# The channel mix over 12 blocks of 384 tokens instead of 9 of 512

## The chip, the core and the metric

The kernel runs on one core of one Trainium2 chip. The metric is the device time of one execution in microseconds (us); lower is better. The core's engines are named as the profile names them: PE (matrix products; PEld is its loading of weights), DVE (vector engine), ACT (scalar engine), POOL and SP, which issues the DMAs.

## The reference, cut to what matters

There are 8 batches of 576 tokens, 8 heads of 64, so a token has 512 channels. Attention goes through 32 packed rows per head, and its output feeds a channel mix:

```python
def attention(q, k, v, p):                 # 8 batches, 8 heads, 576 tokens, 64 wide
    packed = sm_attn(p, k, v)              # 32 packed rows over 576 tokens
    return sm_attn(q, packed, packed)      # 576 tokens over 32 packed rows

def channel_mix(x, mu_k, mu_r, w_k, w_v, w_r):     # x: 8 x 576 tokens x 512 channels
    x_prev = shifted_by_one_token(x)               # zeros ahead of each batch
    xk = mu_k * x + (1 - mu_k) * x_prev
    xr = mu_r * x + (1 - mu_r) * x_prev
    k = maximum(xk @ w_k, 0)                       # 512 -> 1024
    v = (k * k) @ w_v                              # 1024 -> 512
    return sigmoid(xr @ w_r) * v
```

## The kernel before, in words

**Precision.** Every operand of the mix's three products is kept as two fp32r parts, high and low, and every product is three matmuls: high x high, high x low, low x high. The weights are split once (`convert`, L267 to L299): DVE does the integer steps L287, L289, L291 and the subtraction L297, ACT does L285 and L295. There are 20 such pieces: 4 of w_r, 8 of w_k, 8 of w_v.

**Attention, batch by batch.** `loads` and `transposed` bring k and q (L364 on DVE, or L387 on PE for the first two batches), `front` and `weights_of` make the packed rows (L437, L504, L510, L520, L461, L476), and `back` (L541, L553 to L576, L584) makes the batch's output, which ACT copies to SBUF (L606). Attention's DVE rows are mostly 576 elements wide and do not depend on the block of the mix.

**The mix, block by block.** The 4608 tokens are one row of tokens, cut into NB blocks of TB tokens, across the borders of batches. A block i needs every batch of which it holds a token:

- `mix` makes xr and xk, four chunks of 128 channels each: a product with mu on ACT (L639), a multiply-add on DVE (L643), both in one piece for each batch that the block holds; then `split` makes the two parts, ACT L659 and DVE L661.
- `gates`: for each of NT = TB / 128 tiles of tokens, 4 chunks x 3 matmuls (L717 to L719). The 128 tokens are the weights that PE loads, the 512 output channels stream, so a matmul is 128x512 whatever TB is. ACT makes the sigmoid (L728).
- `keys`: for each of 8 tiles of 128 hidden channels, 4 chunks x 3 matmuls (L678 to L680). Here the 128 hidden channels are the weights and the TB tokens stream, so a matmul is 128 x TB. `squared` follows: ACT relu L689 and square L692, DVE L696 and L698.
- `values`: 8 hidden tiles x NT token tiles x 3 matmuls of 128x512 (L746 to L748); `done` multiplies by the gate on DVE (L757) and writes 128 tokens out.

PE's order for a block is gates, keys, values; the mix of block i + 1 is begun when the keys of block i are done (`channel_mix`, L763 to L771).

**What sets the order.** Nothing is scheduled by the hardware beyond each engine's queue. `Flow` plans the program as it is built: every part (a Python generator) names the engine and an assumed duration for its next instruction (`pe(0.69)` for three matmuls), and the planner records whichever part can start first, with ranks for ties. Each engine then executes its own list strictly in that order and waits where an input is missing. So assumed durations choose an order, and the chip's durations decide the time. Until the last gate tile of block 0 is planned, PE gets filler products (L817) in planned gaps.

**Buffers around the change.** Four buffers `xk`, eight `sq` (for squared keys, xr and staged weights), four `tmp` of 512, four `sig`, and four PSUM banks `m` for the products of the mix.

Of the kernel before, what the change touches and what calls it, by code (L numbers as in the profile page):

```python
# [163 lines left out]
def attn_pack_channel_mix(ctx: ExitStack, tc: tile.TileContext, q, k, v, p, mu_k, mu_r, w_k, w_v, w_r, out):  # L164
    nc = tc.nc
    B, H, S, D = q.shape
    NP = p.shape[2]
    DM, DF = w_k.shape
# [5 lines left out]
    NQ = 4 * P  # L174
    NC = DM // P
    NF = DF // P
    TB = 512
    NB = B * S // TB
    NT = TB // P
    WP = 512  # L180
# [21 lines left out]
    def pe(us, after=None):  # L202
        return "tensor", us, after, None
# [29 lines left out]
    def tile_(shape, dtype, tag, slot, name=None):  # L233
        return sb.tile(shape, dtype, name=name or tag, tag=f"{tag}{slot}")
# [7 lines left out]
        for j in range(2 if tag != "free" else 1):  # L242
            const.tile([P, 1 if "m" == tag[0] or "n" == tag[0] else 2], F32, name=f"{tag}{j}", tag=f"{tag}{j}")
    for tag, n, size in (
        ("xk", NC, 2 * TB), ("sq", NF, 2 * TB), ("tmp", 4, WP), ("sig", 4, DM), ("kq", 4, S), ("a", 2, S),
        ("raw", 3, S), ("a2", 1, S), ("e", 2, S), ("aT", 1, 5 * P), ("vt", 2, NPR * 4 * D),
    ):
        for j in range(n):
            sb.tile([P, size], F32, name=tag, tag=f"{tag}{j}")
# [365 lines left out]
    def pieces(i):  # L615
        t, end = i * TB, (i + 1) * TB
        while t < end:
            b, s = divmod(t, S)
            n = min(S - s, end - t)
            yield b, s, n, t - i * TB  # L620
            t += n
# [3 lines left out]
    def mix(i, j, res, tag):  # L625
# [3 lines left out]
        for c in range(NC):  # L629
# [4 lines left out]
            sx = yield from flow.take(space)  # L634
            x32 = tile_([P, TB], F32, space, sx, "x32")
            ready = flow.t
# [31 lines left out]
    def keys(i):  # L668
        for f in range(NF):
            slot = yield from flow.take("m")  # L670
            ph = ps.tile([P, 512], F32, name="ph", tag=f"m{slot}")[:, :TB]
            fs = slice(f * P, (f + 1) * P)
            for c in range(NC):
                yield from flow.wait(("xk", i, c), ("wk", c, f * P // WP * WP))
                yield pe(0.69)
                flow.now.t -= flow.LAG
                _, xh, xl = xks[i, c]
                nc.tensor.matmul(ph, wk_h[:, c, fs], xh, start=(c == 0), stop=False)  # L678
                nc.tensor.matmul(ph, wk_h[:, c, fs], xl, start=False, stop=False)  # L679
                nc.tensor.matmul(ph, wk_l[:, c, fs], xh, start=False, stop=(c == NC - 1))  # L680
                if f == NF - 1:
                    flow.give("xk", xks.pop((i, c))[0])
            flow.spawn(squared(i, f, slot, ph), 0, flow.t + flow.LAG)

    def squared(i, f, slot, ph):
        sr = yield from flow.take("tmp")
        r = tile_([P, WP], F32, "tmp", sr, "r")[:, :TB]
        yield act(TB)
        nc.scalar.activation(r, ph, AF.Relu)  # L689
        flow.give("m", slot)  # L690
        yield act(TB)
        nc.scalar.activation(r, r, AF.Square)  # L692
        sh = yield from flow.take("sq")
        hl = tile_([P, 2, TB], F32R, "sq", sh)
        yield vec2(TB)
        nc.vector.tensor_copy(hl[:, 0, :], r)  # L696
        yield vec(TB)
        nc.vector.tensor_tensor(hl[:, 1, :], r, hl[:, 0, :].bitcast(F32), op=ALU.subtract)  # L698
        flow.give("tmp", sr)
        sqs[i, f] = sh, hl  # L700
        flow.set(("sq", i, f))
# [61 lines left out]
    def channel_mix():  # L763
        for i in range(NB):
            if i == 0:
                mixes(i)
            yield from gates(i)
            yield from keys(i)
            if i + 1 < NB:
                mixes(i + 1)  # L770
            yield from values(i)  # L771
# [74 lines left out]
```

## Time and profile before

| what | before |
| --- | --- |
| median of 3 runs | 606.17 us (605.31 to 607.71) |
| span of the profiled execution, first to last instruction | 605.1 us |
| median less that span | 1.1 us |
| mean granted PE clock | 0.997 |
| PE busy | 593.7 us (98%) |
| DVE busy | 363.9 us (60%) |
| ACT busy | 331.0 us (55%) |
| matmuls of the mix | 2160, all of them 128x512 |

The profiled execution has no separate time of its own beside its span, so the 1.1 us stands for what lies around it. Times in the trace count from the first instruction. A timeline row gives the start, the length of the merged run, the engine, the line, the operation, output <- inputs, the shape and the count; brackets give idle time before it and what ended that. A matmul's length in such a row is its way through the pipeline: the distance between two starts is what it costs in a stream. A row of stretches gives for each engine its busy time and its number of instructions, then the granted PE clock.

### The profile page before, as it was taken

What the parts mean: (1) busy time and instruction counts of PE and PEld (TensorE: products, weight loads), DVE (VectorE), ACT (ScalarE), POOL (GpSimd) and SP (SyncE); (2) the same over time, 40 slices, a digit from 0 to 9 for tenths busy, and PEclk for the clock granted to TensorE, in tenths of its full rate; (3) what the DMA queues carried; (4) which work ended last, traced back from release to release, by engine and by line L of the source; (5) the groups of instructions that cost most, each with busy time, mean ns of one, the idle gap of its engine ahead of it and who ended that gap; (6) DMA issues with size and microseconds to landing.
All of it is one profiled execution on the core that took longest, in us unless ns stands there. A gap on an engine that the chain in (4) does not pass through costs nothing.

```text
span 605.1 us, 10174 instructions
## 1 busy us (share of the span) xinstructions
PE 593.7 (98%) x3984; PEld 471.1 (78%) x3984; DVE 363.9 (60%) x701; ACT 331.0 (55%) x579; POOL 2.1 (0%) x23
## 2 busy tenths in 40 slices
PE   8899999999999999999999999999999999999997
PEld 7787777777777777777877787778788888888886
DVE  1499999949688479556765577166503822451321
ACT  4478784775774648454845485457534803641420
POOL 0000000000000000000000000000000000000000
PEclk9899999999999999999999999999999999999999
DMA  8895561764634646346034702000010010001001
GB/s 189 248 266 136 216 155 34 166 126 88 113 60 137 118 70 139 99 74 143 1 103 64 144 1 72 20 1 0 26 45 1 0 70 0 2 0 71 0 2 69
DMA packets 159184, 49.43 MB, mean 82 GB/s; under 512 B 143776, under 2 KB 151968, under 8 KB 159136
## 3 DMA queue, kind: packets, MB, share of 16 engines
q1 hardware_dynamic: 159136, 48.79, 34.0%
q8 instruction: 31, 0.51, 0.3%
q14 instruction: 17, 0.14, 0.1%
HBM read 39.33 MB, written 9.44 MB: 81 GB/s over the span
## 4 chain that ended last, share of the span: by engine, by line
PE 84%; DVE 5%; ACT 4%; SPq 3%; DMA 2%; issue 1%; ACTq 0%
PE pvo L746 11%; PE ph L678 10%; PE pvo L747 10%; PE pvo L748 10%; PE ph L680 10%; PE ph L679 10%; PE pr L717 5%; PE pr L719 5%; PE pr L718 5%; SPq L207 3%; PE pa L461 2%; PE pa L584 2%; DMA st<-in_moe_w_r 1%; PE pa L541 1%; ACT x L639 1%; DVE m L289 1%
## 5 line engine op out<-in xcount | busy, mean ns | idle before, releaser
L678 PE MATMUL ph<-xk,wk_h 128*128 128x512 f32 x288 | 114.8, 399 | 0.0
L746 PE MATMUL pvo<-wv_h,sq 128*128 128x512 f32 x288 | 113.9, 395 | 0.0
L679 PE MATMUL ph<-xk,wk_h 128*128 128x512 f32 x288 | 112.4, 390 | 0.0
L680 PE MATMUL ph<-xk,wk_l 128*128 128x512 f32 x288 | 112.3, 390 | 0.0
L747 PE MATMUL pvo<-wv_l,sq 128*128 128x512 f32 x288 | 112.3, 390 | 0.0
L748 PE MATMUL pvo<-wv_h,sq 128*128 128x512 f32 x288 | 112.2, 390 | 0.0
L689 ACT ACTIVATE r<-ph 128x512 f32<-128x512 f32 x72 | 43.0, 598 | 90.7 <-PE ph L680 89.7
L696 DVE CAST sq<-r 128x512 fp32r<-128x512 f32 x72 | 30.3, 420 | 100.6 <-ACT r L692 98.4
L746 PEld LDWEIGHTS pvo<-wv_h,sq 128*128 128x128 f32 x288 | 54.1, 188 | 15.9 <-issue 4.5
L678 PEld LDWEIGHTS ph<-xk,wk_h 128*128 128x128 f32 x288 | 54.1, 188 | 15.5 <-issue 4.5
L643 DVE SCALAR_TENSOR_TENSOR x<-xt,mus,x 128x512 f32<-128x512 f32 (+7 forms) x128 | 60.4, 513 | 6.0 <-ACT x L639 5.9
L680 PEld LDWEIGHTS ph<-xk,wk_l 128*128 128x128 f32 x288 | 54.1, 188 | 11.5
L748 PEld LDWEIGHTS pvo<-wv_h,sq 128*128 128x128 f32 x288 | 54.1, 188 | 11.4
L639 ACT ACTIVATE x<-xt,mus 128x512 f32<-128x512 f32 (+7 forms) x128 | 62.0, 530 | 1.5 <-DVE xr L661 1.3
L747 PEld LDWEIGHTS pvo<-wv_l,sq 128*128 128x128 f32 x288 | 54.1, 188 | 10.7
L679 PEld LDWEIGHTS ph<-xk,wk_h 128*128 128x128 f32 x288 | 54.2, 188 | 10.3
L717 PE MATMUL pr<-wr_h,xr 128*128 128x512 f32 x144 | 58.7, 408 | 0.0
L719 PE MATMUL pr<-wr_h,xr 128*128 128x512 f32 x144 | 56.7, 394 | 1.0 <-DVE xr L661 1.0
L718 PE MATMUL pr<-wr_l,xr 128*128 128x512 f32 x144 | 56.3, 391 | 0.0
L728 ACT ACTIVATE sig<-pr 128x512 f32<-128x512 f32 x36 | 21.3, 601 | 60.1 <-PE pr L719 56.5
L698 DVE TENSOR_TENSOR sq<-r,sq 128x512 fp32r<-128x512 f32 x72 | 49.4, 686 | 1.4
L757 DVE TENSOR_TENSOR sig<-pvo,sig 128x512 f32<-128x512 f32 x36 | 23.9, 686 | 38.8 <-PE pvo L748 38.8
(80 smaller groups left out, 727.5 us busy)
## 6 DMA issues: line engine op xcount, KB each, us to landing
out<-sig SPq DMA_DIRECT2D x36, 256.0 KB, 2.1
vt<-in_v SPq DMA_DIRECT2D x16, 512.0 KB, 4.6
raw<-in_k SPq DMA_DIRECT2D x96, 72.0 KB, 2.8
raw<-in_q SPq DMA_DIRECT2D x96, 72.0 KB, 2.8
st<-in_moe_w_k SPq DMA_DIRECT2D x8, 512.0 KB, 6.0
st<-in_moe_w_v SPq DMA_DIRECT2D x8, 512.0 KB, 5.5
raw<-in_k SPq DMA_DIRECT2D x16, 144.0 KB, 2.9
raw<-in_q SPq DMA_DIRECT2D x16, 144.0 KB, 5.1
```

The lines of the kernel that those rows point to most:

```text
L639: nc.scalar.mul(x32[:, o:o + n], xts[b, c][:, 1 + s:1 + s + n], mus[:, j, c:c + 1])
L643: nc.vector.scalar_tensor_tensor(x32[:, o:o + n], xts[b, c][:, s:s + n], mus[:, j + 1, c:c + 1], x32[:, o:o + n], op0=ALU.mult, op1=ALU.add,)
L678: nc.tensor.matmul(ph, wk_h[:, c, fs], xh, start=(c == 0), stop=False)
L679: nc.tensor.matmul(ph, wk_h[:, c, fs], xl, start=False, stop=False)
L680: nc.tensor.matmul(ph, wk_l[:, c, fs], xh, start=False, stop=(c == NC - 1))
L698: nc.vector.tensor_tensor(hl[:, 1, :], r, hl[:, 0, :].bitcast(F32), op=ALU.subtract)
L717: nc.tensor.matmul(pr, xh[:, ts_], wr_h[:, c, :], start=(c == 0), stop=False)
L718: nc.tensor.matmul(pr, xh[:, ts_], wr_l[:, c, :], start=False, stop=False)
L719: nc.tensor.matmul(pr, xl[:, ts_], wr_h[:, c, :], start=False, stop=(c == NC - 1))
L746: nc.tensor.matmul(pv[t], sh, wv_h[:, f, :], start=(f == 0), stop=False)
L747: nc.tensor.matmul(pv[t], sh, wv_l[:, f, :], start=False, stop=False)
L748: nc.tensor.matmul(pv[t], sl, wv_h[:, f, :], start=False, stop=(f == NF - 1))
```

## The change

TB goes from 512 to 384, so there are 12 blocks instead of 9, with 3 tiles of tokens instead of 4. The size of the `sq` buffers is now written with WP, which is 512 as before, since weights are staged there too; the `xk` buffers become 768 wide instead of 1024. The planner's assumed time for three matmuls of the keys goes from 0.69 to 0.52.

```diff
-    TB = 512
+    TB = 384
...
-        ("xk", NC, 2 * TB), ("sq", NF, 2 * TB), ("tmp", 4, WP), ("sig", 4, DM), ("kq", 4, S), ("a", 2, S),
+        ("xk", NC, 2 * TB), ("sq", NF, 2 * WP), ("tmp", 4, WP), ("sig", 4, DM), ("kq", 4, S), ("a", 2, S),
...
-                yield pe(0.69)
+                yield pe(0.52)
```

Counts: gates and values keep 432 and 864 matmuls of 128x512; keys go from 864 of 128x512 to 1152 of 128x384. The rows of `mix` keep their number, because 9 blocks and 12 blocks both cut the batches into 16 pieces; `split` and `squared` go from 72 to 96 rows for each of their instructions. Block 0 lies in batch 0 in both kernels, and block 1 holds tokens of batches 0 and 1 in both: tokens 512 to 1023 before, 384 to 767 now.

On DVE, at the place where block 1's xr is finished, the four chunks of xr before are xr_1359, xr_1390, xr_1426 and xr_1481; x32 is the mixed fp32 chunk, xt_1293 the second half of batch 1's attention output, xt_547 that of batch 0. Before, the end of that stretch reads:

```order
L757 TENSOR_TENSOR sig_728<-pvo_1214,sig_728 128x512
L757 TENSOR_TENSOR sig_751<-pvo_1219,sig_751 128x512
L643 SCALAR_TENSOR_TENSOR x32_1427<-xt_547,mus_111,x32_1427 128x64
L643 SCALAR_TENSOR_TENSOR x32_1427<-xt_1293,mus_111,x32_1427 128x448
L661 TENSOR_TENSOR xr_1426<-x32_1397,xr_1426 128x512
L757 TENSOR_TENSOR sig_774<-pvo_1225,sig_774 128x512
L757 TENSOR_TENSOR sig_802<-pvo_1231,sig_802 128x512
L661 TENSOR_TENSOR xr_1481<-x32_1427,xr_1481 128x512
```

The same place on DVE now, where the chunks of xr are xr_1355, xr_1374, xr_1395 and xr_1435:

```order
L661 TENSOR_TENSOR xr_1395<-x32_1375,xr_1395 128x384
L643 SCALAR_TENSOR_TENSOR x32_1398<-xt_547,mus_111,x32_1398 128x192
L643 SCALAR_TENSOR_TENSOR x32_1398<-xt_1300,mus_111,x32_1398 128x192
L661 TENSOR_TENSOR xk_1380<-x32_1330,xk_1380 128x384
L643 SCALAR_TENSOR_TENSOR x32_1429<-xt_547,mus_111,x32_1429 128x192
L643 SCALAR_TENSOR_TENSOR x32_1429<-xt_1300,mus_111,x32_1429 128x192
L661 TENSOR_TENSOR xr_1435<-x32_1398,xr_1435 128x384
```

The products with the gates (L757) have moved ahead of this piece, there are three of them, and the pieces are 192 + 192 instead of 64 + 448. Counted from the first L643 of block 0 up to and with the last L661 of block 1's xr, DVE's list has 146 rows before and 145 now: the same kinds in the same numbers (all the weight conversions and batch 1's whole attention among them), except for one L757.

On PE, at the passage from block 0 to block 1, the list now reads as follows; sq_1167 is the eighth and last squared tile of block 0, pa the scores of batch 2's attention:

```order
L746 MATMUL pvo_1033<-wv_h_121,sq_1167 128x512
L747 MATMUL pvo_1033<-wv_l_122,sq_1167 128x512
L748 MATMUL pvo_1033<-wv_h_121,sq_1167 128x512
L717 MATMUL pr_1363<-wr_h_119,xr_1355 128x512
L718 MATMUL pr_1363<-wr_l_120,xr_1355 128x512
L719 MATMUL pr_1363<-wr_h_119,xr_1355 128x512
L437 MATMUL pa_1399<-kT_1226,pt_1093 32x288
```

Before, the scores of batch 2 (L437) stood ahead of the last six matmuls of block 0's values; now they stand behind the first three matmuls of block 1's gates, in front of its chunks 1 to 3.

## The prediction

> **What bounds the kernel now.** I read the page first, then the stretches of PE's and DVE's timelines where the blocks meet, and last the groups by shape. The page's span, engine totals and two of its rows of 40 slices (a digit is a tenth of a slice of 15.1 us):
>
> ```profile
> span 605.1 us, 10174 instructions
> ...
> PE 593.7 (98%) x3984; PEld 471.1 (78%) x3984; DVE 363.9 (60%) x701; ACT 331.0 (55%) x579; POOL 2.1 (0%) x23
> ...
> PE   8899999999999999999999999999999999999997
> ...
> DVE  1499999949688479556765577166503822451321
> ```
>
> PE is full nearly throughout. DVE is at 60% on average, but full in slices 3 to 7: in that stage two engines are full together, and a change that lets PE ask earlier there meets DVE.
>
> What a matmul costs on PE is the distance of starts. First and last of the 96 keys matmuls of a late block:
>
> ```profile
> 503.28 0.39 PE L678 MATMUL ph<-xk,wk_h 128*128 128x512 f32 x1
> ...
> 524.82 0.39 PE L680 MATMUL ph<-xk,wk_l 128*128 128x512 f32 x1
> ```
>
> 21.54 us over 95 steps is 0.2267 us each, and not the 0.39 of a single row.
>
> Now the early stage: the first L643 of block 0 on DVE, the end of block 1's xr, and all engines in the stretch from the start of the first to the end of the last (DVE is the third "busy" column).
>
> ```profile
> 42.42 0.74 DVE L643 SCALAR_TENSOR_TENSOR x<-xt,mus,x 128x512 f32<-128x512 f32 x1
> ...
> 119.03 1.29 DVE L757 TENSOR_TENSOR sig<-pvo,sig 128x512 f32<-128x512 f32 x2
> 120.23 0.69 DVE L661 TENSOR_TENSOR xr<-x,xr 128x512 fp32r<-128x512 f32 x1
> ```
> ```profile
> 42.42:120.92 78.50, 75.98 (x551) 58.58 (x549) 76.83 (x148) 59.12 (x109) 0.10 (x1) 1.00 0.55 149
> ```
>
> DVE is busy for 76.83 of 78.50 us: for this whole stretch it works without a pause, on weights, on batch 1's attention and on the mix. PE at the same place, and its last matmul:
>
> ```profile
> 53.35 0.40 PE L717 MATMUL pr<-wr_h,xr 128*128 128x512 f32 x1
> ...
> 118.34 0.39 PE L748 MATMUL pvo<-wv_h,sq 128*128 128x512 f32 x1
> 118.56 0.39 PE L717 MATMUL pr<-wr_h,xr 128*128 128x512 f32 x1
> ...
> 120.60 0.39 PE L717 MATMUL pr<-wr_h,xr 128*128 128x512 f32 x1
> ...
> 600.98 0.39 PE L748 MATMUL pvo<-wv_h,sq 128*128 128x512 f32 x1
> ```
>
> PE finishes block 0 and takes up block 1 at 118.56; chunk 3 of xr is wanted at 120.60 and ends on DVE at 120.92. The two arrive together, with nothing to spare. At the next block there is plenty: the last chunk of block 2's xr on DVE, and PE's first use of that block.
>
> ```profile
> 176.62 0.69 DVE L661 TENSOR_TENSOR xr<-x,xr 128x512 fp32r<-128x512 f32 x1
> ...
> 186.19 0.39 PE L717 MATMUL pr<-wr_h,xr 128*128 128x512 f32 x1
> ```
>
> So from 121 us on PE alone sets the end, and before that it rides on DVE by chance of length: block 0 of 512 tokens is just as long as DVE needs.
>
> **The change part by part.** The forecast is built at one point, the end of block 1's last xr chunk on DVE: when it comes, and what PE has left behind it.
>
> First, when it comes. DVE's list up to there has 145 rows instead of 146, smaller ones and one L757 fewer. The groups by shape (busy, mean ns of one):
>
> ```profile
> L643 DVE SCALAR_TENSOR_TENSOR x<-xt,mus,x 128x512 f32<-128x512 f32 x16 | 11.7, 747 | 0.9 <-ACT x L639 0.9
> L643 DVE SCALAR_TENSOR_TENSOR x<-xt,mus,x 128x448 f32<-128x448 f32 x16 | 10.9, 682 | 0.2 <-ACT x L639 0.2
> L643 DVE SCALAR_TENSOR_TENSOR x<-xt,mus,x 128x384 f32<-128x384 f32 x16 | 9.8, 615 | 0.8 <-ACT x L639 0.8
> L643 DVE SCALAR_TENSOR_TENSOR x<-xt,mus,x 128x192 f32<-128x192 f32 x16 | 6.5, 407 | 0.9 <-ACT x L639 0.9
> L643 DVE SCALAR_TENSOR_TENSOR x<-xt,mus,x 128x64 f32<-128x64 f32 x16 | 4.4, 277 | 0.6 <-ACT x L639 0.6
> L661 DVE TENSOR_TENSOR xr<-x,xr 128x512 fp32r<-128x512 f32 x36 | 24.8, 688 | 1.1 <-ACT xr L659 0.7
> L698 DVE TENSOR_TENSOR sq<-r,sq 128x512 fp32r<-128x512 f32 x72 | 49.4, 686 | 1.4
> L696 DVE CAST sq<-r 128x512 fp32r<-128x512 f32 x72 | 30.3, 420 | 100.6 <-ACT r L692 98.4
> ```
>
> Eight L643 of block 0 shrink by 747 - 615 = 132 ns, 1.06 us; seven pairs of block 1 from 682 + 277 to 2 x 407, 1.02 us. L661 and L698 have no row at 384; they run at L643's length at 512, so I take its step of 132: 13 L661 give 1.72 and 8 L698 1.06. L696 is shorter per element, half the step (bounds nothing and 132 ns): 8 x 66 = 0.53. One L757 fewer is 0.6, since two stood within 1.29. Sum 6.0 us: the chunk ends at 114.9. Bounds: if the 1.67 us of idle time in the stretch go too, 113.2; if DVE waits for PE at the three L757, which now stand ahead of xr chunk 0 and so hold back everything behind them, I allow 3 us: 118.
>
> The rest of that stretch changes nothing here: PE's shorter keys and ACT's shorter rows (ACT 59.12 of 78.50) lie beside DVE, and SP's loads of weights go on when DVE has used a staged piece, so they keep DVE's pace. PE now waits inside block 0 as well, for weights that DVE still converts, but the sum counts from the one point where all these waits have ended. Behind the waiting gates on PE stand the rest of block 1's gates and batch 2's transposes (L520); DVE's squares of block 1 wait for PE in turn, and nothing before the point does.
>
> Second, what is left for PE. Before, 3 chunks of tile 0 are issued by then, so 39 gates + 96 keys + 96 values + 7 blocks of 240 = 1911 matmuls: 433.2 us. Now it is 27 gates + 72 values + 10 x 108 = 1179 of 512 columns, 267.3 us, and 11 x 96 = 1056 keys of 384. Their price is not in the trace. Below it cannot well go under three quarters of 0.2267, 0.170; above, the nearest row is a weight load, which has to fit beside each matmul (mean ns of one, 188):
>
> ```profile
> L678 PEld LDWEIGHTS ph<-xk,wk_h 128*128 128x128 f32 x288 | 54.1, 188 | 15.5 <-issue 4.5
> L387 PEld LDWEIGHTS pa<-ident,raw 96*128 96x128 f32 x72 | 7.1, 140 | 1.4 <-issue 0.3 <-DVE m L289 0.3
> ...
> 5.03 0.66 PE L387 MATMUL pa<-ident,raw 96*128 96x96 f32 x6
> ```
>
> The fp32 products of L387 are 96 columns wide and start (0.66 - 0.25) / 5 = 0.082 us apart, 0.85 ns a column (0.25 is the length of one). If a column of fp32r takes half of that, 512 take 0.219 and 0.008 of each 0.2267 does not shrink with the columns: 0.172 at 384. I take 0.173, near the lower bound: 182.7 us. PE's remaining mix is then 450.0 instead of 433.2, **+16.8 us**. Attention's matmuls of batches 2 to 7 are the same in both; L437 of batch 2 lies ahead of the point in both. So the sum is +16.8 - 6.0 = +10.8.
>
> The Trainium skill, "TensorE: Matmul & The Clock Gate", section "Back-to-back issue gap", gives columns / 2.4 GHz + 2.5 ns, 215.8 ns at 512 and 162.5 at 384; by it the +16.8 would be +13.6. The trace disagrees at 512 with 227.
>
> Third, the clock. PE will stand idle in pieces of 2 to 3 us on its way there, and after such a pause the trace shows half the clock (PE is the first column, the granted clock the third number from the end):
>
> ```profile
> 14.40:16.60 2.20, 0.10 (x1) 0.00 (x0) 0.00 (x0) 0.20 (x2) 0.00 (x0) 1.00 0.50 112
> 18.20:21.60 3.40, 3.40 (x54) 2.82 (x53) 0.00 (x0) 1.97 (x6) 0.00 (x0) 0.50 0.96 268
> ```
>
> 3.40 us at 0.50 lose 1.7 us. One such window falling after the restart is **+1.7**; bounds 0 (it falls into waiting) and 3.4 (two of them). The same page, section "What's actually happening", has the clock halve after an idle window of some 3.4 us; by that rule a pause of 2 us need not halve it, and the term could be 0, but here 2.2 idle us were followed by it.
>
> Sum: 16.8 - 6.0 + 1.7 = **+12.5 us**. The span goes from 605.1 to 617.6; the runs lie 1.1 above the span, so 606.17 + 12.5 = **618.7**. The tail behind the last matmul stays: one L757 and a DMA.
>
> A cross-check from PE's side: block 0 loses 36 matmuls of 0.2267 and 96 x 0.054, so 13.3 us, and starts some 1.4 earlier (14 smaller L643 and L661, less one xk row now ahead of xr's last chunk). PE would take up block 1 near 104 and want chunk 3 near 106; it comes at 114.9. The wait is some 9 us, the keys' extra price over all 12 blocks 1152 x 0.173 - 864 x 0.2267 = 3.4, the start -1.4: +11.
>
> Later blocks: xr's slots come free as values proceed, 4 hidden tiles into them, which leaves 4 tiles x 0.68 = 2.7 us less between xr and its use. The margin at block 2 was 186.19 - 177.31 = 8.9, so about 6 remain: no wait. Batch 2 is first needed by block 3 now, at token 1152 instead of 1024. Costed at nothing.
>
> **The rivals.**
>
> *PE is not held up.* DVE's stretch would end by 106, 9 us ahead of my count, by its rows running closer together once they are no longer spread among PE's longer block. Then only the keys' price and the start count: +3.4 - 1.4 = +2.0, 608.2, no change by the bound below. For it: PE now delivers the keys that DVE squares earlier and closer together. Against it: 1.67 us of idle time is all that DVE has to give. It decides if DVE's stretch falls from 78.5 to under 64 us. Chance 0.08.
>
> *The weight load binds the keys.* If a matmul can't start sooner than 188 ns after the last: 1056 x 0.015 = +15.8 more, 634.5. Against it: L387's loads last 140 ns and their matmuls follow at 82, so loads overlap. Chance 0.05.
>
> *Later blocks lose their margin too.* Were the 8.9 us eaten by shorter values and more rows of fixed cost on DVE and ACT, ten blocks would wait 1.5 each: +15, 633.7. Against it: DVE's 5s and 6s after slice 8. Chance 0.04.
>
> *Everything small at once*, no wait and keys at 0.170: below 603. Chance 0.02.
>
> **How the numbers follow.** The main case has 0.81. Its low end: keys at 0.170 (-3.2), no half clock (-1.7), DVE's idle time gone (-1.7): 612. Its high end: DVE waiting for PE (+3), a second half-clock window (+1.7), keys 3 ns dearer (+3.2): 626. That range leaves out the rivals' 0.19. A measurement here can tell about 0.5% (3 us) from no change: faster 0.02, same 0.08 (the first rival), slower 0.90.
>
> **What would show it.** In the profile after: DVE's L661 for xr of block 1, last chunk, ends near 115, and PE's gates of block 1 wait for it; PE has some 10 us of idle time between 57 and 116 and next to none later; keys start 0.173 apart. If PE takes up block 1 before 107 without waiting, or keys come at 0.188, or waits recur at every block, I am wrong in the way of that rival.

## The result and the profile after

The kernel with 12 blocks of 384 tokens takes 621.34 us (median of 4 runs, 620.86 to 622.45), the kernel before beside it 606.29 us (605.31 to 607.71, 4 runs). The ratio is 1.0251, 95% interval 1.0233 to 1.0268: 15.0 us slower, where 12.5 were forecast. The profiled execution took 621.66 us with a span of 619.9, 14.8 above the span of before (605.1). That execution's time lies 1.8 us above its span; the 1.1 given for before is a median less the span of one execution, and falls out of the difference that was forecast.

First the page after, as it was read of before: the span, the engines' totals, and the rows of 40 slices (now 15.5 us each) of PE, DVE and the granted clock.

```profile
span 619.9 us, 10908 instructions
...
PE 602.6 (97%) x4262; PEld 509.7 (82%) x4262; DVE 370.7 (60%) x773; ACT 340.6 (55%) x649; POOL 2.1 (0%) x23
...
PE   8989998799999999999999999999999999999997
...
DVE  1599979869648756818828924655525427236231
...
PEclk9999998899999999999999999999999999999999
```

Counted from 0, PE has an 8 and a 7 in slices 6 and 7 (93 to 124 us), where it was full before, and the clock sinks in the same two; from slice 8 on it is as full as it was. DVE has a 7 in slice 5 (77 to 93 us): it is no longer busy through the whole early stage.

The key matmuls of a late block, first and last of 96:

```profile
500.14 0.33 PE L678 MATMUL ph<-xk,wk_h 128*128 128x384 f32 x1
...
516.63 0.34 PE L680 MATMUL ph<-xk,wk_l 128*128 128x384 f32 x1
```

16.49 us over 95 steps is 0.1736 us, against 0.2267 at 512 columns.

Now the place where the prediction was made, the end of block 1's xr. On DVE, the row of its last chunk, and the stretch from the first L643 of block 0 to that end (DVE is the third busy column):

```profile
116.84 0.55 DVE L661 TENSOR_TENSOR xr<-x,xr 128x384 fp32r<-128x384 f32 x1
```
```profile
41.49:117.39 75.90, 67.39 (x506) 51.02 (x504) 70.67 (x147) 54.00 (x108) 0.10 (x1) 0.96 0.56 155
102.30:105.70 3.40, 3.40 (x22) 2.17 (x22) 3.40 (x7) 1.80 (x3) 0.00 (x0) 0.50 0.02 5
112.60:116.00 3.40, 3.40 (x34) 1.62 (x23) 3.40 (x10) 2.96 (x9) 0.10 (x1) 0.50 0.94 258
```

The chunk ends at 117.39 instead of 120.92. DVE is busy for 70.67 us, 6.16 less than the 76.83 of before, but idle for 5.23 where it was idle for 1.67. The other two rows are the two stretches of half clock; both lie ahead of the point. PE's timeline there, with its waits in brackets, and its last matmul:

```profile
97.01 0.50 PE L747 MATMUL pvo<-wv_l,sq 128*128 128x512 f32 x1 [1.54 <-DVE wv_l L297]
...
99.66 0.51 PE L746 MATMUL pvo<-wv_h,sq 128*128 128x512 f32 x1 [0.54 <-ACT wv_h L295]
100.93 0.50 PE L747 MATMUL pvo<-wv_l,sq 128*128 128x512 f32 x1 [0.76 <-DVE wv_l L297]
...
108.07 0.40 PE L748 MATMUL pvo<-wv_h,sq 128*128 128x512 f32 x1
109.95 0.50 PE L717 MATMUL pr<-wr_h,xr 128*128 128x512 f32 x1 [1.49 <-ACT xr L659]
110.29 0.40 PE L718 MATMUL pr<-wr_l,xr 128*128 128x512 f32 x1
111.94 0.50 PE L719 MATMUL pr<-wr_h,xr 128*128 128x512 f32 x1 [1.26 <-DVE xr L661]
112.38 2.71 PE L437 MATMUL pa<-kT,pt 64*32 64x288 f32 x32
...
615.31 0.39 PE L748 MATMUL pvo<-wv_h,sq 128*128 128x512 f32 x1
```

PE waits in two places: inside block 0's values for the parts of w_v, and at the gates of block 1 for xr. Before, it was full there. Between 57 and 116 us PE is idle for 7.6 us (some 10 were forecast; before, 1.5), and from there to 615 us for 0.5.

To say where a kernel's time goes I add up, from the trace, what PE loses: for every two successive matmuls the distance of their starts less the median distance of that line, where it is over 0.06 us. Waits, changes of form and half clock are all in it. Beside it stands the first gate matmul of block 0 (us):

| kernel | first gate | lost 40 to 130 | lost 130 to 200 | lost after 200 |
| --- | --- | --- | --- | --- |
| before | 44.7 | 11.1 | 8.8 | 20.3 |
| after | 43.4 | 24.0 | 8.2 | 20.1 |

So the start brings 1.3 back, the early stage costs 12.9 more, everything behind 130 us costs nothing (-0.6, -0.2), and the keys 1152 x 0.1736 - 864 x 0.2267 = 4.1. Together 14.9, and the spans differ by 14.8. The same account is given for nine of the experiments. Where a kernel has two block sizes, the median of a keys line mixes two lengths, and the column of 40 to 130 comes out too large; with a median for each form it is 9.1 for before, 20.5 for after, 9.5 for e1, 9.1 for e5 and 22.6 for e2.

### The profile page after: what moved, and what is told of

Same layout as the page of the kernel before. It is cut to its first block, busy times and chain, and to the rows that moved or that the text cites. A ratio compares the mean times of both kernels' runs of the same rounds, so it can differ in the third digit from the quotient of the medians.

```text
span 619.9 us, 10908 instructions
## 1 busy us (share of the span) xinstructions
PE 602.6 (97%) x4262; PEld 509.7 (82%) x4262; DVE 370.7 (60%) x773; ACT 340.6 (55%) x649; POOL 2.1 (0%) x23
## 4 chain that ended last, share of the span: by engine, by line
PE 82%; DVE 8%; SPq 4%; DMA 2%; ACT 2%; issue 1%; DVEq 0%; ACTq 0%
PE ph L678 10%; PE pvo L746 10%; PE ph L680 10%; PE pvo L747 10%; PE ph L679 10%; PE pvo L748 10%; PE pr L717 5%; PE pr L719 5%; PE pr L718 5%; SPq L207 4%; PE pa L461 2%; PE pa L584 1%; DMA st<-in_moe_w_r 1%; DVE m L289 1%; PE pa L520 1%
## 5 line engine op out<-in xcount | busy, mean ns | idle before, releaser
L678 PE MATMUL ph<-xk,wk_h 128*128 128x384 f32 x384 | 130.6, 340 | 0.0
L680 PE MATMUL ph<-xk,wk_l 128*128 128x384 f32 x384 | 129.0, 336 | 1.0 <-DVE wk_l L297 1.0
L679 PE MATMUL ph<-xk,wk_h 128*128 128x384 f32 x384 | 128.6, 335 | 0.0
L689 ACT ACTIVATE r<-ph 128x384 f32<-128x384 f32 x96 | 47.1, 491 | 89.3 <-PE ph L680 87.2
L696 DVE CAST sq<-r 128x384 fp32r<-128x384 f32 x96 | 33.9, 354 | 103.5 <-ACT r L692 98.7
L678 PEld LDWEIGHTS ph<-xk,wk_h 128*128 128x128 f32 x384 | 72.1, 188 | 5.6 <-issue 3.7
L680 PEld LDWEIGHTS ph<-xk,wk_l 128*128 128x128 f32 x384 | 72.1, 188 | 1.6 <-DVE wk_l L297 1.6
L679 PEld LDWEIGHTS ph<-xk,wk_h 128*128 128x128 f32 x384 | 72.2, 188 | 0.4
L639 ACT ACTIVATE x<-xt,mus 128x384 f32<-128x384 f32 (+1 forms) x128 | 63.7, 529 | 5.4 <-DVE sq L698 4.0
L643 DVE SCALAR_TENSOR_TENSOR x<-xt,mus,x 128x384 f32<-128x384 f32 (+1 forms) x128 | 62.3, 511 | 7.3 <-ACT x L639 6.9
L717 PE MATMUL pr<-wr_h,xr 128*128 128x512 f32 x144 | 59.1, 410 | 1.5 <-ACT xr L659 1.5
L728 ACT ACTIVATE sig<-pr 128x512 f32<-128x512 f32 x36 | 21.3, 601 | 69.5 <-PE pr L719 67.1
L719 PE MATMUL pr<-wr_h,xr 128*128 128x512 f32 x144 | 56.9, 395 | 2.2 <-DVE xr L661 2.0
L698 DVE TENSOR_TENSOR sq<-r,sq 128x384 fp32r<-128x384 f32 x96 | 52.9, 551 | 1.7
L692 ACT ACTIVATE r<-r 128x384 f32<-128x384 f32 x96 | 50.3, 524 | 2.3
```

The lines of the kernel that those rows point to most:

```text
L639: nc.scalar.mul(x32[:, o:o + n], xts[b, c][:, 1 + s:1 + s + n], mus[:, j, c:c + 1])
L643: nc.vector.scalar_tensor_tensor(x32[:, o:o + n], xts[b, c][:, s:s + n], mus[:, j + 1, c:c + 1], x32[:, o:o + n], op0=ALU.mult, op1=ALU.add,)
L717: nc.tensor.matmul(pr, xh[:, ts_], wr_h[:, c, :], start=(c == 0), stop=False)
L719: nc.tensor.matmul(pr, xl[:, ts_], wr_h[:, c, :], start=False, stop=(c == NC - 1))
```

## The experiments

**Where the short blocks cost (e1, e2, e5).** In these kernels the blocks have sizes of their own; each use of TB and NT takes the size of its block. Their lines stand one to three further down than in the kernel before (L719 is the gates' L717, L662 is L661). The edit for e1; the others differ in the list.

```diff
-    TB = 384
-    NB = B * S // TB
+    SIZES = [512] + 8 * [384] + 2 * [512]     # e1
+    SIZES = [384] + 6 * [512] + 3 * [384]     # e2
+    SIZES = 3 * [512] + 8 * [384]             # e5
```

> The blocks are 512, then 8 of 384, then 2 of 512 (11 blocks); block 0 is as before, and two thirds of the tokens stay in blocks of 384. Theory (the loss is one wait at block 1, because DVE's early chain has a length of its own and block 0 is now shorter than it): no such wait, only the price of the narrower keys, 8 x 96 x 0.1735 - 6 x 96 x 0.2267 = +2.7 us, so 609. Rival (every block of 384 pays its share of the +15, by fixed costs per row or by small waits): 8 of 12 shares, +10, so 616.

> The mirror image: blocks of 384, then 6 of 512, then 3 of 384 (10 blocks). Only a third of the tokens lie in blocks of 384, but block 0 is one of them. Theory (one wait at block 1): nearly the whole loss. The last xr chunk of block 1 comes some 1.7 us later than after the change (117.4), since block 1 is larger, and 447.9 us of mix are left for PE instead of 433.2: +12.9 from before by that sum, and about 1 more as the change itself measured over its own sum: 619 to 620. Rival (each block of 384 pays its share): 4 of 12 shares, +5, so 611.

> The first three blocks have 512 tokens (blocks 0 to 2 as in the kernel before, so every batch is due no earlier than there), the other eight have 384. Theory (a wait of one place: PE meets DVE where the early stage ends, and the only standing price of 384 is 3.2 us per thousand keys matmuls): blocks 0 to 2 pass as before, no wait at block 1 or 2, and the eight blocks cost 768 x 0.1735 - 576 x 0.2267 = 2.7 us more in keys: 606.3 + 2.7 = 609, 608 to 610.5. Rival (every block of 384 brings its share of the loss, 8 of 12): 616.

Measured: e1 614.03 us, ratio 1.0135 (1.0114 to 1.0156); e2 621.84, 1.0264 (1.0231 to 1.0297); e5 609.51, 1.0039 (1.0021 to 1.0056).

| kernel | first gate | lost 40 to 130 | lost 130 to 200 | lost after 200 |
| --- | --- | --- | --- | --- |
| e1: 512 first, then 384 | 43.6 | 13.3 | 13.2 | 20.7 |
| e2: 384 first, then 512 | 42.3 | 25.5 | 9.5 | 19.2 |
| e5: 512 three times, then 384 | 44.7 | 12.7 | 10.1 | 21.9 |

e2 has only a third of its tokens in blocks of 384 and the whole loss (619 to 620 were expected); e5 has two thirds of them there and loses what the keys cost (2.7 us; measured 2.4 by the ratio). So blocks of 384 behind the early stage cost next to nothing but their keys, and with a first block of 384 the whole loss is there. e1 missed, and lies nearer to the rival's 616 than to the theory's 609: the wait at block 1 is gone as the theory said, but a new one stands at block 2, where its gates wait for xr chunk by chunk (PE's timeline of e1):

```profile
170.87 0.32 PE L462 MATMUL pa<-vl,aT 64*32 64x64 f32 x8 [1.06 <-ACT aT L529]
...
173.50 0.50 PE L719 MATMUL pr<-wr_h,xr 128*128 128x512 f32 x1 [0.71 <-ACT xr L660]
...
175.71 0.50 PE L719 MATMUL pr<-wr_h,xr 128*128 128x512 f32 x1 [0.79 <-ACT xr L660]
```

With this cut, block 2 begins at token 896 and holds the first tokens of batch 2 (from 1152), which before were first needed from block 2 at 1024 and after from block 3 at 1152. From this I took the token at which a block first needs a new batch for the cause. That theory fell later (e10, e11).

**DVE's work made less, first try (e3, e4).** The conversion of w_v leaves out its integer steps and its subtraction on DVE, with their planned slots; ACT copies stand in their place. w_v's two parts are then plain copies of the staged words.

```diff
+        if hi is wv_h:
+            yield act(n)
+            nc.scalar.copy(hi[:, c, o:o + n], w1.bitcast(F32))
+            yield act(n)
+            nc.scalar.copy(lo[:, c, o:o + n], w1.bitcast(F32))
...
+            return
```

> The changed kernel, with DVE relieved: both parts of w_v are copied by ACT straight from the staged words, so the 3 bit operations and the subtraction of 8 pieces (some 2.1 us each, 17 us) are left out on DVE. PE's work is unchanged; the values use wrong weights. Theory (DVE's chain holds up block 1): the chain ends near 100, ahead of PE, so the wait goes: 606.3 + 4.0 (keys) - 2.4 (earlier start) + 0.7 (waits of w_k that stay) = 608.6, that is 12 to 13 below the changed kernel. Rival (each block pays): still near 620.

> The kernel before with the same part left out (both parts of w_v are plain copies by ACT). Theory: PE and DVE met at block 1 with nothing to spare, and PE sets the time, so taking 17 us from DVE gains no more than the small waits after 53 us: 605 to 606. With the run of the changed kernel beside it the difference between the block sizes should shrink from 15 to 3 or 4 us. Rival (each block pays): the difference stays near 15. A third view (before, DVE's early chain was already the bound): this one gains 5 us or more, under 601.

Measured: e3 627.57 us, ratio 1.0351 (1.0322 to 1.0380); e4 615.07, 1.0152 (1.0128 to 1.0177). Both missed, and both are slower than the kernels that do the whole work. The planner, given fewer DVE slots, wrote another order (lines stand ten further down). In e3, batch 2's scores (L447) now stand between the two products of batch 1's output (L594) on PE, and DVE, where batch 1's mix (L653) should come, waits for the load of batch 2's q:

```profile
104.70 1.26 PE L594 MATMUL pa<-a,pm 32*64 32x288 f32 x16 [3.62 <-DVE a L586]
106.69 2.71 PE L447 MATMUL pa<-kT,pt 64*32 64x288 f32 x32 [0.72 <-ACT xt L616]
112.44 2.41 PE L594 MATMUL pa<-a,pm 32*64 32x288 f32 x16 [3.04 <-ACT a L520]
```
```profile
114.40 0.78 DVE L374 STREAM_TRANSPOSE qT<-raw 128x576 f32<-128x576 f32 x1 [2.14 <-DMA raw<-in_q]
...
117.98 1.36 DVE L653 SCALAR_TENSOR_TENSOR x<-xt,mus,x 128x192 f32<-128x192 f32 x4
```

These runs can't tell what DVE's work is worth, since the order moved with it.

**The same with the order kept (e6, e7).** Every planned slot and every instruction stays, only the four DVE rows of each w_v piece get 32 columns instead of 512 (and the low part of w_v is zeroed by POOL at the start).

```diff
-    wv_l = const.tile([P, NF, DM], F32R, name="wv_l")
+    wv_l = const.tile([P, NF, DM], F32R, name="wv_l"); nc.gpsimd.memset(wv_l.bitcast(F32), 0.0)
...
-        nc.vector.tensor_scalar(m, m, 3, None, op0=ALU.logical_shift_left)
+        d = 32 if lo is wv_l else n; nc.vector.tensor_scalar(m[:, :d], m[:, :d], 3, None, op0=ALU.logical_shift_left)
...
```

> The changed kernel, with every instruction in its place, but the four DVE rows of each of the eight pieces of w_v do 32 columns instead of 512, so the rest of the low part of w_v stays zero; some 8 x 4 x 0.5 us = 16 us less work on DVE before block 1. Theory (DVE's work up to block 1's xr is what PE waits for): the last xr chunk of block 1 comes before PE wants it, the wait inside block 0's values goes as well, and what stays is the keys' price +3.4 and the earlier start -1.4 to -2.4: 607 to 609; up to 611 if batch 1's attention keeps a chain of its own (PE, ACT, DMA) that ends after 106. Rival (the loss comes with the shorter blocks and not from DVE's list): 619 to 621.

> The same 32 columns in the kernel before, order kept. Theory: there DVE and PE arrive together, so taking 16 us off DVE gives back only the small waits for weights inside block 0: 604.5 to 606, and the difference to the changed kernel of the same kind is 2 to 4 us where it was 15. Rival (the loss is elsewhere): the difference stays 13 to 15.

Measured: e6 618.34 us, ratio 1.0184 (1.0162 to 1.0206); e7 606.64, 1.0004 (0.9990 to 1.0017).

| kernel | first gate | lost 40 to 130 | lost 130 to 200 | lost after 200 |
| --- | --- | --- | --- | --- |
| e6: after, thin w_v | 44.3 | 20.8 | 7.0 | 20.0 |
| e7: before, thin w_v | 44.3 | 10.9 | 9.1 | 20.0 |

e7 gained nothing: 606.64 beside 606.62 is a little above the 604.5 to 606 that were expected. e6 missed: DVE's total fell by 13.0 us (370.7 to 357.7 on the pages, 16 were expected), and 3.0 of them arrived by the medians, 4.1 by the ratios. The pair differs by 11.7 us, nearer to the rival's 13 to 15 than to the theory's 2 to 4. What DVE does in e6 between 69.5 and 90.9 us (third busy column), what PE does there (first), and what ends DVE's idle time:

```profile
69.50:90.90 21.40, 21.35 (x225) 17.68 (x227) 9.91 (x43) 17.20 (x35) 0.00 (x0) 1.00 0.48 119
```
```profile
91.69 1.45 DVE L553 STREAM_TRANSPOSE e<-pa 128x576 f32<-128x576 f32 x2 [2.88 <-PE pa L541]
...
113.12 0.55 DVE L661 TENSOR_TENSOR xr<-x,xr 128x384 fp32r<-128x384 f32 x1
```

DVE is idle for half of that time, and then waits for L541, the scores of batch 1's output; PE is full, and L541 stands in its queue behind the matmuls that fill it. From its first row behind L541 (L553) DVE needs 22.0 us to the end of chunk 3 of xr (113.67), where it needs 25.1 in the changed kernel (92.29 to 117.39): the weights between the rows of the chain are worth only these 3 us. So the theory in its first form, that DVE's list is what PE waits for, fell: it is a chain that goes through PE's own queue.

**Behind L541 (e9).** e6, with four softmax rows of each half of batch 1's output cut to 64 of 576 columns, one of them shown:

```diff
-        nc.vector.tensor_reduce(m2, e, axis=AX.X, op=ALU.max)
+        nc.vector.tensor_reduce(m2[:, :2 * d], e[:, :2 * d], axis=AX.X, op=ALU.max)
```

> The changed kernel with thin w_v rows (32 of 512 columns, as before) and, for batch 1's output alone, the softmax rows L560, L562, L566 to L572 on DVE doing 64 of 576 columns; order kept, so part of w_v's low half and of batch 1's attention is left out. It takes some 4.3 us more off DVE (8 rows of 0.65 to 0.67 us down to about 0.12), all of it between batch 1's L541 and L584. Theory now (the point hangs on batch 1's chain: L437, L541, softmax, L584, L606, then the mix of block 1, and rows of DVE ahead of L541 count only until L541 comes): every us taken behind L541 counts in full, where of the 16 us taken ahead of it and beside it only 3.7 did: the point from 113.7 to about 109.5, time 618.3 - 4.3 = 614, 612 to 615. Rival (PE's own list sets the point, DVE is no longer in it): 617 to 619.

Measured: 616.94 us, ratio 1.0172 (1.0146 to 1.0198), at the rival's edge (617) and above the theory's 615. The account: first gate 43.7, lost 19.3, 7.0, 20.1. The point came at 111.2, 2.5 earlier than in e6 instead of 4.3: L566 waits twice for ACT (0.77 and 0.35), the second half's transpose for PE, the first mix row for ACT, and then the mix of block 1 takes its 9.6 us on DVE without a pause, whatever stood ahead of it. So not all that was taken off DVE came off the chain: steps on ACT and PE then set its pace. The time moved by 1.4 us by the medians and by 0.7 by the ratios, whose intervals overlap; only the trace tells e9 from e6.

```profile
97.91 0.78 DVE L576 STREAM_TRANSPOSE a<-e 128x576 f32<-128x576 f32 x1 [1.25 <-PE pa L584]
...
101.64 0.83 DVE L643 SCALAR_TENSOR_TENSOR x<-xt,mus,x 128x192 f32<-128x192 f32 x2 [0.57 <-ACT x L639]
...
110.66 0.56 DVE L661 TENSOR_TENSOR xr<-x,xr 128x384 fp32r<-128x384 f32 x1
```

**Due tokens (e10, e11).** Block lists again: e10 has `[384, 128] + 8 * [512]`, and e11 is the changed kernel with `TB = 256` (18 blocks) and 0.37 for the planner's three key matmuls. In both, block 1 holds batch 0 alone.

> Blocks of 384, 128 and then eight of 512: block 0 is as short as in the changed kernel, but batch 1 is first needed by block 2, at token 512, as in the kernel before (384 in the changed one). Theory (what counts is from which token on a block needs a new batch, since the batch is ready at a fixed time, not the length of a block): no wait for batch 1; 606.3 plus the keys' price, 96 x (0.1735 + p - 0.2267) with p for 128 columns between 0.067 (the line through 512 and 384) and 0.14 (a load of 0.140): +1.3 to +8.3, I take 610. Rival (a short block 0 costs the wait wherever batch 1 comes in): 619 to 622.

> 18 blocks of 256. Batch 1 is first needed at token 512 and batch 2 at token 1024, as in the kernel before. Theory (due tokens): no wait of over 2 us at block 2 or block 4, only keys: 18 x 96 x p - 864 x 0.2267 with p = 0.1203 on the line through 512 and 384: +12.0, so 618; with p from 0.113 (half of 0.2267) to 0.130: 606 to 635, and the trace gives p and the waits apart. Rival 1 (DVE's rows, more of them with a fixed cost each, make the early stage longer: some 5 us of wait on top): 623 for p = 0.1203. Rival 2 (each block brings its share of the changed kernel's loss, 18 blocks): 650.

Measured: e10 626.74 us, ratio 1.0334 (1.0301 to 1.0366); e11 644.89, 1.0634 (1.0603 to 1.0665).

| kernel | first gate | lost 40 to 130 | lost 130 to 200 | lost after 200 |
| --- | --- | --- | --- | --- |
| e10: 384, 128, then 512 | 42.3 | 21.1 | 14.7 | 21.8 |
| e11: 256 | 42.7 | 42.2 | 8.3 | 20.7 |

The theory of due tokens failed in both: e10 is above even its rival, and e11 lies between its two. The waits stand where no block needs batch 1 yet, inside the values of block 0, at the products of batch 1's output (L585 in e10, L584 in e11) and at w_v:

```profile
97.11 0.39 PE L751 MATMUL pvo<-wv_h,sq 128*128 128x512 f32 x1
104.24 1.27 PE L585 MATMUL pa<-a,pm 32*64 32x288 f32 x16 [6.75 <-DVE a L577]
```
```profile
93.41 0.79 PE L747 MATMUL pvo<-wv_l,sq 128*128 128x512 f32 x1 [4.09 <-DVE wv_l L297]
...
98.03 1.27 PE L584 MATMUL pa<-a,pm 32*64 32x288 f32 x16 [2.12 <-DVE a L576]
...
102.48 1.27 PE L584 MATMUL pa<-a,pm 32*64 32x288 f32 x16 [3.18 <-DVE a L576]
```

Batch 1's attention goes ahead of the mix in the planner's ranks, so its products stand in PE's queue at the place the plan gave them, and PE waits there, with work behind them that doesn't need batch 1. (Whether e1's wait at block 2 is of this kind too was not shown.) The keys' part of the forecast held: 0.1199 us at 256 columns (505.49 to 516.88 over 95 steps below), on the line through 512 and 384, so 1728 x 0.1199 - 195.9 = 11.3 us of e11's 38.

```profile
505.49 0.28 PE L678 MATMUL ph<-xk,wk_h 128*128 128x256 f32 x1
...
516.88 0.28 PE L680 MATMUL ph<-xk,wk_l 128*128 128x256 f32 x1
```

**A subtraction moved to POOL (e8).** A version meant to be faster, with all of the work:

```diff
-        yield vec(n)
-        nc.vector.tensor_tensor(lo[:, c, o:o + n], m.bitcast(F32), hi[:, c, o:o + n].bitcast(F32), op=ALU.subtract)
+        yield pool(n)
+        nc.gpsimd.tensor_tensor(lo[:, c, o:o + n], m.bitcast(F32), hi[:, c, o:o + n].bitcast(F32), op=ALU.subtract)
```

> The changed kernel with the subtraction of all 20 weight pieces moved from DVE to GpSimd, which is idle; nothing is left out, but the planner makes a new order around it. DVE's rows up to the end of block 1's xr fall by some 12 us. Theory: the wait at block 1 shrinks from about 11 us to less than 4: 609 to 614. Rival 1 (GpSimd takes over 1.5 us for a piece, so the low parts of w_v come late and PE waits in block 0 instead): 616 to 622. Rival 2 (the loss comes with the blocks): 621.

Measured: 629.78 us, ratio 1.0371 (1.0346 to 1.0397), outside every range given. POOL needs 1.44 us for a piece, and DVE was not relieved: its total is 376.3 us, against 370.7 in the changed kernel. Of its 20 rows L291, 11 take 1.64 to 1.76 us, where the changed kernel has 0.65 to 0.69; each of the 11 starts while POOL is in a piece, and none of the other nine does. One such pair, from DVE's and POOL's timelines:

```profile
84.96 1.76 DVE L291 SCALAR_TENSOR_TENSOR m<-st,m 128x512 uint32<-128x512 uint32 x1
```
```profile
84.88 1.29 POOL L297 TENSOR_TENSOR wv_l<-m,wv_h 128x512 fp32r<-128x512 f32 x1 [3.85 <-ACT wv_h L295]
```

Here too the planner wrote another order, in which PE stops in the midst of block 0's keys:

```profile
75.34 0.74 PE L387 MATMUL pa<-ident,raw 96*128 96x96 f32 x3 [5.06 <-ACT a L510]
```

**More work in the chain of the kernel before (e12).** One softmax row of batch 1's second half is done nine times:

```diff
-        nc.vector.tensor_reduce(m2, e, axis=AX.X, op=ALU.max)
+        for _ in range(9 if (b, hf) == (1, 1) else 1): nc.vector.tensor_reduce(m2, e, axis=AX.X, op=ALU.max)
```

> The kernel before, with one row of batch 1's softmax (L560 of its second half, 0.66 us) done nine times instead of once: 5.3 us more on DVE, all between batch 1's L541 and L584; order kept, result unchanged. Theory (the kernel before stands just at the kink: DVE has no idle time between 90 and 121 us and chunk 3 of block 1's xr ends 0.3 us after PE could use it, so less DVE work brings nothing, as e7 showed, but more counts in full): the point moves from 120.9 to about 126, the time to 606.5 + 5 = 611.5, 610 to 614 with a half-clock window. Rival (PE's own values, which the L757 ahead of that chunk wait for, set the point, and DVE has several us to give): 606 to 608.

Measured: 614.62 us, ratio 1.0109 (1.0077 to 1.0141): 6.6 us more by the ratio, and just above the 610 to 614 that were expected. DVE's ten rows take 7.67 us instead of the 1.37 of two, so 6.3 were added; PE waits for the chain at L584, and half clock follows:

```profile
94.06 7.67 DVE L560 TENSOR_REDUCE m<-e 128x18 f32<-128x576 f32 x10
```
```profile
108.56 1.27 PE L584 MATMUL pa<-a,pm 32*64 32x288 f32 x16 [5.77 <-DVE z L568]
109.76 0.80 PE L746 MATMUL pvo<-wv_h,sq 128*128 128x512 f32 x1
```

The account: first gate 45.5, lost 19.1, 8.0, 21.9. The expectation had the two engines meet at block 1's xr; the wait came earlier, inside block 0's values. In the kernel before, that product had its input just in time, as the rows of DVE and PE show (L576 ends at 101.69):

```profile
100.92 0.77 DVE L576 STREAM_TRANSPOSE a<-e 128x576 f32<-128x576 f32 x1
```
```profile
101.92 0.74 PE L584 MATMUL pa<-a,pm 32*64 32x288 f32 x16
```

With e7 this shows the edge on which the kernel before stands: 12.4 us less in DVE's total (363.9 to 351.5) bring nothing, 6.3 more in the chain cost all of it.

## Why the prediction was right, and where its reason was only half of it

The direction, the place and the size were right: a wait in the early stage that the 512-token block had covered, and a small standing price for the keys. That the sum came so near is in part luck: two terms were too small by 3.6 us together, and one was too large by 1.7.

- *DVE's rows*: priced at -6.0, measured -6.16 busy time. Right.
- *The point*: forecast at 114.9, came at 117.39. The stretch began 0.93 earlier, the rows took 6.16 less, but idle time went from 1.67 to 5.23. This is the term that was mis-sized: the sum took a full DVE to stay full. DVE now waits for ACT's part of w_v (3.4 us in the two rows below, 1.0 before) and for ACT's first mix product (0.95), which the upper bound of 118 covered, though not by the mechanism it named (the three L757):

```profile
82.89 0.69 DVE L297 TENSOR_TENSOR wv_l<-m,wv_h 128x512 fp32r<-128x512 f32 x1 [2.44 <-ACT wv_h L295]
84.56 0.69 DVE L297 TENSOR_TENSOR wv_l<-m,wv_h 128x512 fp32r<-128x512 f32 x1 [0.97 <-ACT wv_h L295]
...
107.81 0.83 DVE L643 SCALAR_TENSOR_TENSOR x<-xt,mus,x 128x192 f32<-128x192 f32 x2 [0.95 <-ACT x L639]
```

- *What is left for PE*: forecast +16.8, measured from the point to the last matmul 615.31 - 117.39 = 497.92 against 600.98 - 120.92 = 480.06, so +17.9. The keys at 0.1736 instead of 0.173 are 0.6 of the difference, a wait of 0.5 for ACT right behind the point most of the rest.
- *The clock*: +1.7 was set for a window after the restart; none came there. The pauses on the way were to be 2 to 3 us long, and none is longer than 1.54. Both windows fell into the waiting, ahead of the point: behind the first, PE still waits 1.49 us for xr, and behind the second it takes up chunk 3's low part at 117.44, when DVE has just ended it. What the first added to the point by holding up L584 was not taken apart.
- The sum of these, -3.5 + 17.9 and 0.4 at the tail, is the 14.8 of the spans: the point's 2.5 and PE's 1.1 too little, the clock's 1.7 too much.
- *The meeting before*: the prediction set 120.60, where PE wants chunk 3, against 120.92, where DVE ends it. But the row at 120.60 is L717, which reads the high part that ACT makes; the low part from DVE is read by L719 at 121.06. DVE was ahead by 0.14 us and not behind, so the two do arrive together:

```profile
121.06 0.41 PE L719 MATMUL pr<-wr_h,xr 128*128 128x512 f32 x1
```

- *Later blocks* lose nothing (20.1 us after 200 us against 20.3), and the weight loads don't bind the keys. Those two rivals fell, and with them the first one: PE was held up. So did the last, with 621.34 us against its 603.

The reason was half right. The prediction said that PE "rides on DVE by chance of length: block 0 of 512 tokens is just as long as DVE needs". That the first blocks decide it is shown (e2, e5), and that the kernel before has no slack in this chain (e7, e12). But DVE's full list is not the thing waited for: e6 took 13.0 us from DVE and the wait mostly stayed. What both kernels share is L541, the scores of batch 1's output, which PE reaches at the same time. Before:

```profile
91.03 1.20 PE L541 MATMUL pa<-qT,ppT 64*32 64x288 f32 x32
```

After:

```profile
91.06 1.20 PE L541 MATMUL pa<-qT,ppT 64*32 64x288 f32 x32
```

Behind it, until the first gate of block 1, PE's list holds 6 keys, 96 values and 64 small products of attention before, 27.5 us without a wait (118.56 - 91.03). After, it holds 39 values and 32 small products: 39 x 0.2267 = 8.8 and two merged runs of L584, about 10 us. (The 27.5 include L541 itself; with it the 10 become some 11.) The chain from L541 over softmax, L584, ACT's copies and the mix takes 26.3 us to chunk 3 after, 22.8 in e6 and 21.0 in e9 (L541 at 90.20). So some 10 us of work stand against a chain of over 20, and taking rows off DVE shortens the chain by no more than those that stand in it (in e9 by less). The waits for w_v inside block 0's values lie within the same stretch: e6 leaves 0.8 of their 2.8 us, and the time still follows the point. In e10, e11 and e12 the same chain is met earlier, at L584. That reading fits these traces, but it is argued from them; it was not tried by moving batch 1's attention ahead in the order of the changed kernel, so how much of the 12.9 us a new plan for 384 would give back is open. No version tried beats the kernel before.

## What to carry to other kernels

When a block gets smaller, do not price the block; find what the old block's length was covering. Where two engines arrive together, take the row on which both pass (here L541), count what each has left behind it, and the larger of the two sets the time. And a relief that lets a planner write a new order is not an experiment on the relief (e3, e4, e8): keep every slot and shrink what is in it.

## What the hardware showed beyond the forecast

- A key matmul with its own weight load costs 0.2267 us at 512 columns, 0.1736 at 384, 0.1199 at 256: about 0.053 for each 128 columns, and some 0.013 that do not shrink. At 128 columns the line would give 0.067, but three steps from 125.76 to 126.10 in e10 take 0.113 each: there something else binds, and with a load for every matmul the load is the likely one (argued, not shown).

```profile
125.76 0.28 PE L681 MATMUL ph<-xk,wk_l 128*128 128x128 f32 x1
...
126.10 0.27 PE L681 MATMUL ph<-xk,wk_l 128*128 128x128 f32 x1
```

- Half clock came after pauses far shorter than its own 3.40 us. The Trainium skill, "TensorE: Matmul & The Clock Gate", section "What's actually happening", has the clock throttled after an idle window of about 3.4 us; the kernel after has none that long in the early stage, only waits of 1.54 us and less, and was throttled twice. Nor does the length of a pause decide it alone: e6 and e9 have the same two waits at the gates of block 1 (1.25 and 1.26 us, 2 us apart), e6 ran at half clock right behind them from 108.4 to 111.8 us, and e9 did not. The traces do show a difference. In each of them all half-clock stretches between the first matmul and the last start whole steps of 3.413 us apart (102.318 and 112.558 in the kernel after, three steps). Laid on those steps (in e9 counted back from 612.24, where the clock sinks at the end), e6's two waits fall into one step and e9's into two (PE's busy time is the first busy column; the first row is e6, the others e9):

```profile
104.99:108.40 3.41, 0.90 (x3) 0.47 (x3) 3.41 (x8) 2.56 (x8) 0.00 (x0) 1.00 0.79 179
```
```profile
100.25:103.66 3.41, 2.28 (x9) 1.42 (x8) 2.84 (x8) 3.41 (x10) 0.00 (x0) 1.00 0.53 85
103.66:107.07 3.41, 2.03 (x25) 0.85 (x33) 3.41 (x9) 2.45 (x7) 0.00 (x0) 1.00 0.99 303
```

So it seems to be PE's idle time within one such step that counts. Over all runs here, from 20 to 600 us, every step at full clock with 1.75 us or more of idle time was followed by half clock, and none with under 1.25 us was; in between both occur (1.26 us in e3's step from 124.53 was, 1.68 in e11's from 109.17 was not). No run was made to test it.
